# The first two batches of a fused attention and feed-forward kernel: columns of f in runs of four instead of eight

## The chip, the cores and the metric

One core of a Trainium2 chip runs the whole program in one launch. Its engines are TensorE (PE, matrix multiplies), VectorE (DVE), ScalarE (ACT), GpSimd (POOL) and SyncE (SP, which here issues every DMA, in the order of its own queue). The metric is the device time of the launch in microseconds, lower being better. The time before is the median of three runs.

## What is computed

```python
def sm_attn(qq, kk, vv):                    # softmax attention, scale 1/8
    ...
p_packed = sm_attn(p, k, v)                 # 32 packed queries for each head
out      = sm_attn(q, p_packed, p_packed)   # 8 batches, 8 heads, 576 rows, 64 wide
x = out.transpose(0, 2, 1, 3).reshape(4608, 512)
h = x @ w_in                                # 512 -> 2048
g = maximum(h, 0) + alpha * minimum(h, 0)
x = g @ w_out                               # 2048 -> 512
y = (silu(x @ w_gate) * (x @ w_val)) @ w_out2
```

Everything is float32 to the outside. The weights arrive as 64-bit words that the kernel narrows to 32 bits itself, and large products are made of rounded high and low parts in three matmuls.

## The kernel before

There are two stages. The first one goes from q, k, v, p to x after `w_out`, the second is the gated feed-forward. The change lies in the first.

**Units.** A half batch j (288 rows; batch 0 is j = 0 and 1) and a block f of 128 of the 2048 columns make one unit. There are 16 half batches and 16 blocks, so 256 units, numbered `it`. `h_unit` makes the block's h in 6 matmuls, ACT makes `m` (L1003), DVE makes `g` (L1006), ACT rounds it (`hi`, L1014), and POOL takes the rest (`lo`, L1016). Three units later `o_unit` multiplies g into four accumulators `acc` (L1029, L1030, L1035, 12 matmuls), one PSUM bank each, with no second buffer. One DVE instruction on L1006 belongs to each unit, so the rows of L1006 count units.

**Runs.** Consecutive units of one j accumulate in `acc`. When a run ends before f = 15, the sums are copied out (ACT L1051, DVE L1049) and stored to DRAM (`x1p`, SP L1052). The next run of that j loads them back (`load_part`, SP L981) and adds them on DVE as it empties `acc` (L1047). These copies, loads and adds share a pool `x` of two tiles. A run needs both of them, so a load waits until the store of the run ahead has landed. Batches 0 and 1 (j = 0 to 3) go in runs of eight: f 0 to 7 for j = 0, 1, 2, 3 (units 0 to 31), then f 8 to 15 for the same (units 32 to 63). From batch 2 on a run has all sixteen blocks.

**Windows.** h isn't made from x and `w_in` directly: `pp_win(b, j)`, a *window* written `wbj` in the tables, multiplies the packed attention of batch b into four blocks of `w_in` (PE L795 for batches 0 and 1, then an ACT copy and a DVE subtraction, L800, for each half of the heads). It takes two PSUM buffers `at` of which there are two in all. Units of b with f 0 to 3 need window 0, f 4 to 7 window 1, and so on.

**Pieces.** `convert()`, the word `1` in the tables, narrows one of 32 pieces of `w_in` (i0 to i15) and `w_out` (o0 to o15), in the sequence `ORDER`. A piece costs five DVE instructions (L224, L228, L237, L246 and mostly L254), one or two of ACT and one or more of POOL. Window 0 needs i0 to i3, and the units of f need o*f* three units later. Once unit 42 is reached (`GROUP0 = 84`, two slots to a unit), the weights of the second stage are narrowed too, into DRAM (`wgvd`, `wo2d`).

**Order.** `START` and `EARLY` are written by hand: which attention steps (a and b are batch 0, c and d batch 1), pieces and windows stand at which unit. A scheduler makes each engine's queue from that, and each engine works through its queue in order. From unit 32 on each 32 units also carry the attention of the batch that follows.

Of the kernel before, what the change touches and what calls it, by code (L numbers as in the profile page):

```python
# [8 lines left out]
F32 = mybir.dt.float32  # L9
# [8 lines left out]
P = 128  # L18
# [7 lines left out]
LOADS = "b.v a.v 1", "a.q 1 1 b.q"  # L26
START = """
    a.kt0 b.kt0 a.pt a.kt1 b.kt1 b.pt a.s1 a.et a.pp b.s1 a.ppt b.et b.qt0 a.qt0 b.pp b.qt1 a.qt1
    a.s20 b.ppt b.s20 a.a20 b.a20 1 1 1 1 1 w00 1 1
"""  # L30
EARLY = {
    (0, 0): "c.pd d.pd",
    (0, 1): "c.pt 1 b.s21 c.kt0 c.kt1",
    (1, 0): "c.s1",
    (1, 1): "d.kt0 d.pt 1 c.et d.qt0 c.pp",
    (2, 0): "c.qt0",
    (3, 0): "w01 d.qt1 a.s21",
    (3, 1): "c.ppt b.a21",
    (4, 1): "1 d.kt1 d.s1 a.a21 c.qt1",
    (5, 1): "1",  # L40
    (6, 1): "1 d.et",
    (7, 0): "d.pp",
    (7, 1): "1",
    (10, 1): "c.s2 d.ppt d.s2 w10",
    (11, 1): "1",
    (13, 0): "d.a2",
    (15, 0): "c.a2",
    (17, 1): "w11",
    (18, 1): "1 1",
    (20, 1): "1 1",  # L50
    (21, 1): "1",
    (23, 1): "1",
    (24, 1): "1",
    (25, 1): "1 1",
    (26, 1): "1 1",
    (27, 1): "1 w02",
    (28, 1): "w03",
    (33, 1): "1",
    (36, 1): "w12 w13",
    (37, 1): "1 1",  # L60
}

ORDER = """
    i2 o2 i0 i3 i1 o0 o3 o1 i5 i4 i7 i6 o5 o4 o7 o6
    i13 i10 i11 o13 i15 i8 i14 i9 i12 o10 o14 o8 o9 o12 o11 o15
"""

BEHIND = {"c.k": 3, "c.q": 4, "c.v": 5, "d.k": 5, "d.q": 6, "d.v": 9}

BY_POOL = {0, 2, 4, 7, 11, 18, 23, 29}  # L70
HOLD = {15: 5, 16: 7, 17: 15, 19: 16}


STEPS = """
# [12 lines left out]

GROUP0 = 84  # L90


FIRST_X = dict(load=-36, A11=-27, S=-26, S2=-25, A12=-12, D4=-11, S3=-11, S1=-10, A22=-8, S4=-7)
# [11 lines left out]
def f32(ap):  # L105
    return ap.bitcast(F32)
# [3 lines left out]
def tile_kernel(  # L110
# [24 lines left out]
    B, H, S, D = q.shape  # L135
    NP = p.shape[2]
    NT, DM = out.shape
    KC = DM // P
    NF1 = alpha.shape[0] // P
# [6 lines left out]
    HS = S // 2  # L146
    NBLK = NT // (2 * T)
    NQ = H // HQ
    NHALF = 2 * B
# [3 lines left out]
    dram = ctx.enter_context(tc.tile_pool(name="dram", bufs=1, space=DRAM))  # L153
# [16 lines left out]
    def utile(tag, shape, name, dt=F32):  # L170
        return upool.tile(shape, dt, tag=tag, name=name, bufs=UBUFS[tag])
# [32 lines left out]
    def like(ap, other):  # L204

        return ap if len(other.shape) == 2 else ap.rearrange("p (c f) -> p c f", c=KC)
# [4 lines left out]
    def use(*cut):  # L211
        raws[:] = sum((r for r, _ in cut), [])
        vals[:] = sum((v for _, v in cut), [])

    def widen(src, raw, val, out=None, n_piece=-1):
# [3 lines left out]
        low, high = words[:, :, 0], words[:, :, 1]  # L219
        held = n_piece in HOLD  # L220
        with tc.issue_after(begun[HOLD[n_piece]].ins) if held else ExitStack():
            nc.scalar.activation(out=f32(val), in_=f32(high), func=AF.Abs)
# [46 lines left out]
    def convert(n=1):  # L269

        for src, parts, f in queue[:n]:
            raw, val = raws.pop(0), vals.pop(0)
            raws.append(raw)
            vals.append(val)
            n_piece = len(issued)
            dst = parts()
            light = len(dst) == 1
            for _ in widen(src, raw, val, dst[0] if light else None, n_piece):
                pass
            if not light:  # L280
                hi, lo = dst
                full = like(f32(val), hi)
                nc.scalar.activation(out=full, in_=full, func=AF.Copy, scale=sg[:, f : f + 1])
                nc.scalar.activation(out=hi, in_=full, func=AF.Copy)
                nc.gpsimd.tensor_tensor(out=lo, in0=full, in1=f32(hi), op=ALU.subtract)
        del queue[:n]
# [7 lines left out]
    def cut_up(t, raws):  # L294

        n = t.shape[1]
        return (
            [t[:, 1024 * i : 1024 * (i + 1)] for i in range(raws)],
            [t[:, c : c + 512] for c in range(1024 * raws, n, 512)],
        )  # L300
# [248 lines left out]
    def behind():  # L549

        return tc.issue_after(before[-1].ins) if before else ExitStack()

    def done(last):
        if chained:
            before[:] = [last]
# [250 lines left out]
    for f in range(NF1):  # L806
# [4 lines left out]
    space = cut_up(raw_tiles[0], 2), cut_up(raw_tiles[1], 1)  # L811
# [3 lines left out]
        a=quad(0),  # L815
        b=quad(1, ["h"], evac=nc.vector),
        c=quad(2),
        d=quad(3, ["h", "at"]),
# [9 lines left out]
    def run(script):  # L828
        for word in script.split():
            if word == "1":  # L830
                convert()
            elif word[0] == "w":
                pp_win(int(word[1]), int(word[2]))
            else:
                n, step = word.split(".")
                if step == "pd":
                    groups[n][step](pd[:, dense[n][0], :], dense[n][1])
                else:
                    groups[n][step]()

    def alphas():
# [6 lines left out]
        nc.vector.tensor_tensor(out=sal, in0=sg, in1=al, op=ALU.mult)  # L848

    run("a.k")  # L850
    nc.sync.dma_start(out=pd, in_=p[0:2].rearrange("b (g h) n d -> (h n) (b g) d", g=2))
    run("b.k a.pd b.pd")
    for i, words in enumerate(LOADS):
        run(words)
        if i == 0:
            alphas()
    run(START)
    for word, i in BEHIND.items():
        with tc.issue_after(issued[i].ins):
# [6 lines left out]
    def at(it, late, fn):  # L866

        plan.setdefault((it, late), []).append(fn)

    order = []
    for bs in [(0, 1)] + [(b,) for b in range(2, B)]:
        for fs in (range(NF1 // 2), range(NF1 // 2, NF1)) if len(bs) > 1 else (range(NF1),):
            for j in range(2 * bs[0], 2 * bs[-1] + 2):
                order += [(j, f, f == fs[0], f == fs[-1]) for f in fs]

    NB1 = 2 * NF1
    busy = set()
# [3 lines left out]
    for b in range(2, B):  # L883
        d0 = 2 * NB1 * (b - 1)
        steps_of = attention(b)
        for entry in STEPS.split():
            d, names = entry.split(":")
# [74 lines left out]
    def more_weights2(vector):  # L962

        for _ in range(2):
            if not kinds:
                kinds.append(next(work2, None))
            if kinds[0] is None or kinds[0] == "v" and not vector:
                return
            vector = vector and kinds[0] == "p"
            kinds[:] = [next(work2, None)]  # L970
# [5 lines left out]
    x1p = {}  # L976

    def load_part(j):
        part[j] = [utile("x", [P, 2, HS], f"x1p{j}_{pr}") for pr in range(2)]
        for pr in range(2):  # L980
            nc.sync.dma_start(out=part[j][pr], in_=x1p[j][:, 2 * pr : 2 * pr + 2, :])  # L981
# [37 lines left out]
    def o_unit(it):  # L1019
        j, f, start, stop = order[it]  # L1020
        ghi, glo = gs.pop(it)
        hi, lo = wout[f // WP]
        for dc in range(KC):
            if start:
                acc[dc] = ps.tile([P, 512], F32, tag=f"acc{dc}", name=f"acc{dc}_{it}")[:, :HS]
        with behind():
            for dc in range(KC):
                c = slice(dc * P, (dc + 1) * P)
                nc.tensor.matmul(acc[dc], lo[:, f % WP, c], ghi, start=start, stop=False)  # L1029
                last = nc.tensor.matmul(acc[dc], hi[:, f % WP, c], ghi, start=False, stop=False)  # L1030
        done(last)
        with behind():
            for dc in range(KC):
                c = slice(dc * P, (dc + 1) * P)
                last = nc.tensor.matmul(acc[dc], hi[:, f % WP, c], glo, start=False, stop=stop)  # L1035
        done(last)
        if not stop:
            return
        if f != NF1 - 1:
            x1p[j] = dram.tile([P, KC, HS], F32, name=f"x1p{j}")  # L1040
        dst = x1d[j] if f == NF1 - 1 else x1p[j]
        for pr in range(2):
            xs = part[j][pr] if j in part else utile("x", [P, 2, HS], f"x1s{it}_{pr}")
            for i in range(2):
                a = acc[2 * pr + i]
                if j in part:
                    nc.vector.tensor_tensor(out=xs[:, i, :], in0=a, in1=xs[:, i, :], op=ALU.add)  # L1047
                elif i:
                    nc.vector.tensor_copy(out=xs[:, i, :], in_=a)  # L1049
                else:  # L1050
                    nc.scalar.activation(out=xs[:, i, :], in_=a, func=AF.Copy)  # L1051
            nc.sync.dma_start(out=dst[:, 2 * pr : 2 * pr + 2, :], in_=xs)  # L1052

    for j in range(4):
        at(NB1 + 8 * j + 6, 0, lambda j=j: load_part(j))


    raw2, xs2, gvw, wo2, ps2, acc2, outs = {}, {}, {}, {}, {}, {}, {}
# [229 lines left out]
    def steps(it, late):  # L1288


        with ExitStack() as held:
# [6 lines left out]
            slot = 2 * it + late  # L1298
            if slot >= GROUP0:
                more_weights2(slot not in busy)  # L1300
# [59 lines left out]
```

## Time and profile before

| | us |
|---|---|
| median of 3 runs (1701.03 to 1706.88) | 1701.05 |
| profiled execution | 1702.91 |
| its span, first to last instruction | 1701.1 |
| outside the span | 1.8 |

Over the span PE is busy 95%, DVE 51%, ACT 40%, POOL 42%. The average hides that the stretches differ. Until 60.6 us no unit has finished its `g`. The 256 units end at 855 us, the second stage fills the rest. A busy PE isn't PE at its peak: matmuls follow each other every 0.13 us, while the profile gives each about 0.30 us, so a short wait leaves no gap in the row.

### The profile page before, as it was taken

The page shows a single profiled execution, that of the slowest core. Times are in us where ns is not written, and L with a number is a line of the kernel's source. Part 1 is how long each engine was busy: PE and PEld are TensorE (multiplying, and loading weights), DVE is VectorE, ACT ScalarE, POOL GpSimd, SP SyncE. Part 2 cuts the span into 40 slices and gives each one's busy share as a digit, 9 for nine tenths or more (in the row PEclk, how much of TensorE's full clock was granted, in tenths as well). Part 3 has the DMA queues.
Part 4 walks back from the last instruction along what each step waited for, and adds up shares of the span by engine and source line. Part 5 has one row for each costly group of instructions (what it writes and reads, how often), then busy time and mean ns, then how long its engine had stood idle before and what let it go on. Part 6 is the DMA issues. An engine that isn't in the chain of part 4 may idle for free.

```text
span 1701.1 us, 28474 instructions
## 1 busy us (share of the span) xinstructions
PE 1609.9 (95%) x10708; PEld 1456.6 (86%) x10708; DVE 868.2 (51%) x1549; ACT 683.0 (40%) x1511; POOL 708.8 (42%) x752
## 2 busy tenths in 40 slices
PE   5688899999999989999899999999999999999997
PEld 3467798988888888889899999999999999999997
DVE  6999757565756656565533443443443343244222
ACT  5774645555544555454522232232232232123122
POOL 3556744565554654547622322322322222232222
PEclk7799999999999999999999999999999999999999
DMA  9433464635445362644573463465455456445442
GB/s 238 121 102 115 120 159 115 165 95 155 130 108 143 117 156 53 150 138 139 182 274 141 177 237 139 166 202 185 164 211 182 158 191 202 159 174 185 156 173 81
DMA packets 227369, 266.11 MB, mean 156 GB/s; under 512 B 130464, under 2 KB 189856, under 8 KB 227232
## 3 DMA queue, kind: packets, MB, share of 16 engines
q1 hardware_dynamic: 227232, 264.30, 49.2%
q8 instruction: 84, 1.38, 0.3%
q14 instruction: 53, 0.43, 0.1%
HBM read 214.70 MB, written 49.55 MB: 155 GB/s over the span
## 4 chain that ended last, share of the span: by engine, by line
issue 39%; PE 25%; POOL 17%; DMA 7%; DVE 6%; ACT 4%; SPq 1%; POOLq 0%; ACTq 0%; DVEq 0%
POOL pl L1247 8%; PE acc L1029 5%; PE acc L1030 5%; PE acc L1035 5%; POOL s L1227 4%; DMA wgvd<-cva 4%; PE h L305 3%; PE h L307 2%; PE h L306 2%; POOL lo L1016 1%; DMA cva<-in_moe_w_gate_dram 1%; POOL cva L934 1%; DVE g L1006 1%; PE ppw L564 1%; POOL cva L265 1%
## 5 line engine op out<-in xcount | busy, mean ns | idle before, releaser
L1016 POOL TENSOR_TENSOR lo<-g,hi 128x288 fp32r<-128x288 f32 x256 | 227.5, 890 | 240.6 <-ACT hi L1014 187.8
L1227 POOL TENSOR_TENSOR s<-s,u 128x384 f32<-128x384 f32 x72 | 73.0, 1014 | 489.9 <-ACT s L1221 489.9
L1006 DVE SCALAR_TENSOR_TENSOR g<-h,sg,m 128x288 f32<-128x288 f32 x256 | 130.3, 509 | 162.2 <-ACT m L1003 132.0
L1184 DVE TENSOR_TENSOR u<-yb,p 128x384 f32<-128x384 f32 x144 | 80.1, 556 | 255.6 <-PE yb L307 255.6
L1247 POOL TENSOR_TENSOR pl<-s,ph 128x384 fp32r<-128x384 f32 x144 | 145.5, 1032 | 106.4 <-ACT ph L1245 106.4
L305 PE MATMUL h<-a2h,ppw 128*128 128x288 f32 x512 | 163.2, 319 | 27.0 <-DVE g L1006 21.4
L1184 DVE TENSOR_TENSOR u<-vb,u 128x384 f32<-128x384 f32 x144 | 80.4, 558 | 197.3 <-PE vb L307 196.9
L1014 ACT ACTIVATE hi<-g 128x288 fp32r<-128x288 f32 x256 | 113.1, 442 | 155.5 <-DVE g L1006 149.1
L307 PE MATMUL o<-wp,ph 128*128 128x512 f32 x432 | 171.5, 397 | 0.0
L306 PE MATMUL o<-wp,ph 128*128 128x512 f32 x432 | 170.9, 396 | 0.0
L305 PE MATMUL o<-wp,pl 128*128 128x512 f32 x432 | 168.8, 391 | 0.9 <-POOL pl L1247 0.9
L1221 ACT ACTIVATE s<-p 128x384 f32<-128x384 f32 x72 | 37.9, 526 | 302.0 <-DVE p L1184 302.0
L307 PE MATMUL h<-a2l,ppw 128*128 128x288 f32 x512 | 153.0, 299 | 0.0
L306 PE MATMUL h<-a2h,ppw 128*128 128x288 f32 x512 | 152.5, 298 | 0.0
L305 PEld LDWEIGHTS h<-a2h,ppw 128*128 128x128 f32 x512 | 97.9, 191 | 62.4 <-DVE g L1006 33.0
L305 PE MATMUL yb<-ring,gv 128*128 128x384 f32 x432 | 146.0, 338 | 0.2
L307 PE MATMUL yb<-ring,gv 128*128 128x384 f32 x432 | 144.4, 334 | 0.0
L306 PE MATMUL yb<-ring,gv 128*128 128x384 f32 x432 | 144.4, 334 | 0.0
L1003 ACT ACTIVATE m<-h,sal 128x288 f32<-128x288 f32 x256 | 125.6, 492 | 41.5 <-PE h L307 40.6
L1245 ACT ACTIVATE ph<-s 128x384 fp32r<-128x384 f32 x144 | 69.8, 519 | 121.3 <-DVE s L1225 121.3
L307 PEld LDWEIGHTS h<-a2l,ppw 128*128 128x128 f32 x512 | 98.0, 191 | 0.8 <-issue 0.8
L306 PEld LDWEIGHTS h<-a2h,ppw 128*128 128x128 f32 x512 | 98.4, 192 | 0.0
(232 smaller groups left out, 4187.1 us busy)
## 6 DMA issues: line engine op xcount, KB each, us to landing
gv<-wgvd SPq DMA_DIRECT2D x144, 896.0 KB, 6.2
wgvd<-cva SPq DMA_DIRECT2D x84, 256.0 KB, 2.6
cva<-in_moe_w_out_dram SPq DMA_DIRECT2D x28, 512.0 KB, 3.8
v<-in_v_dram SPq DMA_DIRECT2D x16, 576.0 KB, 5.4
out_dram<-os SPq DMA_DIRECT2D x12, 768.0 KB, 3.8
cva<-in_moe_w_in_dram SPq DMA_DIRECT2D x16, 512.0 KB, 3.9
kr<-in_k_dram SPq DMA_DIRECT2D x96, 72.0 KB, 2.8
qr<-in_q_dram SPq DMA_DIRECT2D x96, 72.0 KB, 2.5
```

Source lines behind the costliest of these rows:

```text
L305: nc.tensor.matmul(o, wlo, xhi, start=start, stop=False, **kw)
L306: nc.tensor.matmul(o, whi, xhi, start=False, stop=False, **kw)
L307: return nc.tensor.matmul(o, whi, xlo, start=False, stop=stop, **kw)
L1003: begun[it] = nc.scalar.activation(out=m, in_=hp, func=AF.Copy, scale=sal[:, f : f + 1])
L1006: made[it] = nc.vector.scalar_tensor_tensor(out=g32, in0=hp, scalar=sg[:, f : f + 1], in1=m, op0=ALU.mult, op1=ALU.max)
L1014: rounded[n] = nc.scalar.activation(out=hi, in_=x, func=AF.Copy)
L1016: nc.gpsimd.tensor_tensor(out=lo, in0=x, in1=f32(hi), op=ALU.subtract)
L1029: nc.tensor.matmul(acc[dc], lo[:, f % WP, c], ghi, start=start, stop=False)
L1030: last = nc.tensor.matmul(acc[dc], hi[:, f % WP, c], ghi, start=False, stop=False)
L1184: return nc.vector.tensor_tensor(out=out, in0=bank, in1=x, op=ALU.add)
L1227: latest.append(nc.gpsimd.tensor_tensor(out=s2, in0=s2, in1=u3, op=ALU.mult))
L1247: nc.gpsimd.tensor_tensor(out=lo, in0=x, in1=f32(hi), op=ALU.subtract)
```

## The change

The columns of batches 0 and 1 are taken in other runs, listed in a table `RUNS`. Units 0 to 7 are now f 0 to 3 of j = 0 and 1, units 8 to 15 f 4 to 7 of these. Units 16 to 31 are as before. Units 32 to 47 are f 8 to 11 of j = 0, 1, 2, 3, units 48 to 63 f 12 to 15. A run that isn't the first of its j loads the sums of the run ahead of it, at its own last unit (before: at the seventh of eight). So 10 runs load and add sums where 4 did, and 10 store sums to `x1p` where 4 did.

The tables are rewritten with it. The second half of batch 0's attention (`a.s21`, `a.a21`, `b.a21`) stands some units earlier, since unit 4 uses it now instead of unit 8. Window 1 of batch 0 stands at unit 4 instead of 3, and is needed at unit 8 instead of 4. Windows w03, w12 and w13 stand at units 41, 33 and 50 instead of 28, 36 and 36. The 32 pieces are spread until unit 41 (before: 37). `D` at unit 37 gives up a scratch tile. `GROUP0` is 90, so the second stage's weights begin three units later.

```diff
-    a.s20 b.ppt b.s20 a.a20 b.a20 1 1 1 1 1 w00 1 1
+    a.s20 b.ppt b.s20 a.a20 b.a20 1 1 1 1 1 w00
...
-    (28, 1): "w03",
...
-    (36, 1): "w12 w13",
+    (33, 1): "1 w12",
...
+    (37, 0): "D",
...
+    (41, 1): "1 w03",
...
+    (50, 1): "w13",
...
-    i13 i10 i11 o13 i15 i8 i14 i9 i12 o10 o14 o8 o9 o12 o11 o15
+    i8 i9 i10 i11 o8 o9 o10 o11 i12 i13 i14 i15 o12 o13 o14 o15
...
+RUNS = ((0, 1), 0, 4), ((0, 1), 4, 8), ((2, 3), 0, 8), ((0, 1, 2, 3), 8, 12), ((0, 1, 2, 3), 12, 16)
...
-GROUP0 = 84
+GROUP0 = 90
...
-    order = []
-    for bs in [(0, 1)] + [(b,) for b in range(2, B)]:
-        for fs in (range(NF1 // 2), range(NF1 // 2, NF1)) if len(bs) > 1 else (range(NF1),):
-            for j in range(2 * bs[0], 2 * bs[-1] + 2):
-                order += [(j, f, f == fs[0], f == fs[-1]) for f in fs]
+    order, again = [], []
+    for js, f0, f1 in RUNS + tuple(((j,), 0, NF1) for j in range(4, NHALF)):
+        for j in js:
+            if f0:
+                again.append((len(order) + f1 - f0 - 1, j))
+            order += [(j, f, f == f0, f == f1 - 1) for f in range(f0, f1)]
...
-    for j in range(4):
-        at(NB1 + 8 * j + 6, 0, lambda j=j: load_part(j))
+    for it, j in again:
+        at(it, 0, lambda j=j: load_part(j))
```

Below, names like `g_14` carry the unit; the changed kernel's lines stand 11 to 14 further down (L1049 is L1063, L1047 is L1061, L981 is L995, L1052 is L1066, L795 is L806).

DVE's queue around the end of unit 14, before: `g` of units 14 to 17, pieces in between (`cva`, `cvb`).

```order
L1006 SCALAR_TENSOR_TENSOR g_14_1288<-h_1281,sg,m_1289 128x288
L1006 SCALAR_TENSOR_TENSOR g_15_1325<-h_1318,sg,m_1326 128x288
L224 TENSOR_SCALAR cvb_103<-cvb_103 128x512
L228 TENSOR_SCALAR cvb_103<-cvb_103 128x512
L237 SCALAR_TENSOR_TENSOR cvb_103<-cva_102,cvb_103 128x512
L1006 SCALAR_TENSOR_TENSOR g_16_1352<-h_1345,sg,m_1353 128x288
L224 TENSOR_SCALAR cvb_103<-cvb_103 128x512
L246 TENSOR_SCALAR cva_102<-cvb_103 128x512
L228 TENSOR_SCALAR cvb_103<-cvb_103 128x512
L254 SCALAR_TENSOR_TENSOR cva_102<-cva_102 128x512
L237 SCALAR_TENSOR_TENSOR cvb_103<-cva_101,cvb_103 128x512
L1006 SCALAR_TENSOR_TENSOR g_17_1379<-h_1372,sg,m_1380 128x288
```

The same place of the change, from the last of four additions for the run of units 8 to 11 (`x1p_1_1191`) to the first of four for units 12 to 15 (`x1p_0_1342`):

```order
L1061 TENSOR_TENSOR x1p_1_1191<-acc_8_1236,x1p_1_1191 128x288
L235 TENSOR_SCALAR cvb_103<-cvb_103 128x512
L1020 SCALAR_TENSOR_TENSOR g_15_1353<-h_1346,sg,m_1354 128x288
L239 TENSOR_SCALAR cvb_103<-cvb_103 128x512
L248 SCALAR_TENSOR_TENSOR cvb_103<-cva_102,cvb_103 128x512
L1020 SCALAR_TENSOR_TENSOR g_16_1368<-h_1361,sg,m_1369 128x288
L257 TENSOR_SCALAR cva_102<-cvb_103 128x512
L265 SCALAR_TENSOR_TENSOR cva_102<-cva_102 128x512
L1020 SCALAR_TENSOR_TENSOR g_17_1411<-h_1404,sg,m_1412 128x288
L1061 TENSOR_TENSOR x1p_0_1342<-acc_12_1376,x1p_0_1342 128x288
```

Eight additions stand between `g_14` and `g_18` where two copies stood, the second four only three units behind the first.

SP's queue at that place before, two stores of `x1p` among loads of pieces (`cva`):

```order
L217 DMA cva_101<-in_moe_w_in_dram 128x4x256
L217 DMA cva_102<-in_moe_w_in_dram 128x4x256
L1052 DMA x1p_1455<-x1s_0_1456 128x576
L1052 DMA x1p_1455<-x1s_1_1460 128x576
L217 DMA cva_101<-in_moe_w_in_dram 128x4x256
```

And in the change, where `x1p_7_1325` is the store of the run of units 8 to 11, `x1p_0_1342` and `x1p_1_1343` are the loads for units 12 to 15, and `kr` is batch 2's k:

```order
L1066 DMA x1p_7_1325<-x1p_0_1190 128x576
L603 DMA kr_2_2102<-in_k_dram 32x18x32
L1066 DMA x1p_7_1325<-x1p_1_1191 128x576
L603 DMA kr_2_2102<-in_k_dram 32x18x32 x2
L995 DMA x1p_0_1342<-x1p_3_1181 128x576
L603 DMA kr_2_2102<-in_k_dram 32x18x32
L995 DMA x1p_1_1343<-x1p_3_1181 128x576
```

Between the store of one run and the additions of the next there is now a load that waits for that store.

PE's queue at the windows of batch 1, before, behind the h of unit 36 (`ppw_2` is window 2, `ppw_3` window 3; a row is one half of the heads):

```order
L307 MATMUL h_2085<-a2l_409,ppw_3_1834 128x288
L795 MATMUL ppw_20_2101<-wi_1425,ppT_788 64x512 x2
L795 MATMUL ppw_21_2106<-wi_1425,ppT_1130 64x512 x2
L795 MATMUL ppw_30_2112<-wi_1192,ppT_788 64x512 x2
L795 MATMUL ppw_31_2117<-wi_1192,ppT_1130 64x512 x2
L1029 MATMUL acc_32_2122<-hi_1965,wo2l 128x288
```

In the change, w13 behind the h of unit 50:

```order
L318 MATMUL h_2767<-a2l_409,ppw_3_2360 128x288
L806 MATMUL ppw_30_2783<-wi_1861,ppT_793 64x512 x2
L806 MATMUL ppw_31_2788<-wi_1861,ppT_1143 64x512 x2
L637 MATMUL ppt_2793<-ident,ppbd_94 128x128
L1043 MATMUL acc_44_2682<-hi_2656,wo2l 128x288
```

The two windows of batch 1 stood behind each other and now stand apart, with other work behind each.

## Rows read from the trace of the kernel before

**Rows 1.** Busy time by stretch: length, then busy time and count of each engine.

```profile
core 0: us, PE busy (x) PEld busy (x) DVE busy (x) ACT busy (x) POOL busy (x), PEclk, DMA share, GB/s
60.00:100.00 40.00, 30.14 (x199) 22.87 (x199) 36.75 (x65) 33.57 (x71) 23.44 (x20) 0.96 0.36 108
100.00:140.00 40.00, 36.49 (x258) 29.95 (x257) 35.85 (x63) 24.11 (x54) 25.84 (x23) 1.00 0.31 83
140.00:180.00 40.00, 33.23 (x214) 27.35 (x213) 36.92 (x55) 21.78 (x45) 26.07 (x24) 0.96 0.40 125
180.00:230.00 50.00, 45.00 (x381) 39.48 (x380) 31.91 (x61) 29.16 (x65) 30.07 (x29) 1.00 0.48 125
230.00:286.00 56.00, 55.75 (x508) 49.93 (x507) 37.66 (x69) 28.30 (x64) 29.83 (x34) 1.00 0.58 156
```

**Rows 2.** Waits of DVE, 60 to 180 us: total, times, longest.

```profile
DVE g L1006 <- ACT m L1003: 2.5, 2, 1.9
DVE cvb L224 <- ACT cvb L222: 2.5, 3, 1.5
DVE cva L224 <- ACT cva L222: 2.2, 1, 2.2
```

**Rows 3.** Busy time of L1006 alone (DVE, one a unit), by stretch.

```profile
176.00:286.00 110.00, 18.26 (x37) 1.00 0.52 137
```

**Rows 4.** An addition's duration (min/median/max, ns); then L224, L228, L237, L246, L254 by stretch.

```profile
L1047 DVE TENSOR_TENSOR x1p<-acc,x1p x16: 420/448/457, 223.3 to 295.6; 128x288 f32<-128x288 f32 x16
...
60.00:180.00 120.00, 14.19 (x20) 0.97 0.36 105
...
60.00:180.00 120.00, 17.08 (x20) 0.97 0.36 105
...
60.00:180.00 120.00, 18.16 (x19) 0.97 0.36 105
...
60.00:180.00 120.00, 12.19 (x20) 0.97 0.36 105
...
60.00:180.00 120.00, 14.99 (x17) 0.97 0.36 105
```

**Rows 5.** Timeline of DVE: start, duration; `g` of units 14 and 17.

```profile
131.65 0.50 DVE L1006 SCALAR_TENSOR_TENSOR g<-h,sg,m 128x288 f32<-128x288 f32 x1
...
138.96 0.50 DVE L1006 SCALAR_TENSOR_TENSOR g<-h,sg,m 128x288 f32<-128x288 f32 x1
```

**Rows 6.** Timelines of DVE and SP at three run ends, then L981's time to landing.

```profile
192.48 0.82 DVE L1049 COPY x1s<-acc 128x288 f32<-128x288 f32 x2 [0.24 <-PE acc L1035]
...
199.34 0.48 SPq L981 DMA_DIRECT2D x1p<-x1p  x1
...
223.33 1.54 DVE L1047 TENSOR_TENSOR x1p<-acc,x1p 128x288 f32<-128x288 f32 x4
...
226.31 1.09 SPq L981 DMA_DIRECT2D x1p<-x1p  x2
...
245.16 1.55 DVE L1047 TENSOR_TENSOR x1p<-acc,x1p 128x288 f32<-128x288 f32 x4
...
249.79 1.69 SPq L981 DMA_DIRECT2D x1p<-x1p  x2
...
DMA to landing us min/median/max: 2.7/3.3/5.4
```

**Rows 7.** Timeline of PE at windows w12 and w13; in brackets the idle time ahead.

```profile
200.04 1.08 PE L795 MATMUL ppw<-wi,ppT 128*64 128x512 f32 x4 [3.05 <-DVE ppw L800]
```

**Rows 8.** Timeline of ACT near the end of the second stage's weights.

```profile
841.05 0.42 ACT L933 ACTIVATE cva<-cva 128x256 fp32r<-128x256 f32 x1 [3.18 <-DMA wgvd<-cva]
```

**Rows 9.** Durations on L228 over the whole span, min/median/max in ns.

```profile
L228 DVE TENSOR_SCALAR cva<-cva x50: 386/426/1539, 16.5 to 828.9; 128x512 uint32<-128x512 uint32 x50
```

**Rows 10.** Waits of PE, 60 to 180 us: total, times, longest.

```profile
PE acc L1029 <- DVE x1s L1049: 3.0, 1, 3.0
```

More of the change, by code (lines that the diff above doesn't have):

```diff
@@ L32 @@
     (0, 0): "c.pd d.pd",
-    (0, 1): "c.pt 1 b.s21 c.kt0 c.kt1",
+    (0, 1): "c.pt 1 b.s21 a.s21 c.kt0 c.kt1",
     (1, 0): "c.s1",
[L35 to L40, printed above, removed]
+    (1, 1): "1 b.a21 d.kt0 d.pt",
+    (2, 0): "a.a21 c.et",
+    (2, 1): "1 c.pp",
+    (3, 0): "d.qt0",
+    (3, 1): "1 c.qt0",
+    (4, 1): "c.ppt d.kt1 w01",
+    (5, 1): "1 d.s1 c.qt1",
     (6, 1): "1 d.et",
     (7, 0): "d.pp",
-    (7, 1): "1",
+    (7, 1): "1 d.qt1",
+    (8, 1): "1",
     (10, 1): "c.s2 d.ppt d.s2 w10",
@@ L48 @@
     (17, 1): "w11",
-    (18, 1): "1 1",
-    (20, 1): "1 1",
+    (18, 1): "1",
+    (20, 1): "1",
     (21, 1): "1",
@@ L53 @@
     (24, 1): "1",
-    (25, 1): "1 1",
-    (26, 1): "1 1",
-    (27, 1): "1 w02",
-    (28, 1): "w03",
-    (33, 1): "1",
-    (36, 1): "w12 w13",
-    (37, 1): "1 1",
+    (25, 1): "1",
+    (26, 1): "w02",
+    (27, 1): "1",
+    (29, 1): "1",
+    (31, 1): "1",
+    (33, 1): "1 w12",
+    (34, 1): "1",
+    (35, 1): "1",
+    (36, 1): "1",
+    (37, 0): "D",
+    (39, 1): "1",
+    (41, 1): "1 w03",
+    (43, 1): "1",
+    (50, 1): "w13",
 }
@@ L64 @@
     i2 o2 i0 i3 i1 o0 o3 o1 i5 i4 i7 i6 o5 o4 o7 o6
-    i13 i10 i11 o13 i15 i8 i14 i9 i12 o10 o14 o8 o9 o12 o11 o15
+    i8 i9 i10 i11 o8 o9 o10 o11 i12 i13 i14 i15 o12 o13 o14 o15
 """
-BEHIND = {"c.k": 3, "c.q": 4, "c.v": 5, "d.k": 5, "d.q": 6, "d.v": 9}
+BEHIND = {"c.k": 3, "c.q": 4, "c.v": 5, "d.k": 5, "d.q": 6, "d.v": 7}
 BY_POOL = {0, 2, 4, 7, 11, 18, 23, 29}
-HOLD = {15: 5, 16: 7, 17: 15, 19: 16}
+HOLD = {17: 15, 19: 18}
+RUNS = ((0, 1), 0, 4), ((0, 1), 4, 8), ((2, 3), 0, 8), ((0, 1, 2, 3), 8, 12), ((0, 1, 2, 3), 12, 16)
 STEPS = """
@@ L831, in run @@
                 convert()
+            elif word == "D":
+                use(*space)
             elif word[0] == "w":
@@ L1039, in o_unit @@
         if f != NF1 - 1:
-            x1p[j] = dram.tile([P, KC, HS], F32, name=f"x1p{j}")
+            x1p[j] = dram.tile([P, KC, HS], F32, name=f"x1p{j}_{f}")
         dst = x1d[j] if f == NF1 - 1 else x1p[j]
```

## The prediction

> **What bounds the kernel now.** I read the busy times by stretch first [rows 1]. The reader is to see two regimes ahead of 286 us. From 60 to 180 us DVE is busy 36.75 + 35.85 + 36.92 = 109.5 of 120 us, 91%, while PE is at 99.9 of 120. From 230 us on PE is busy 55.75 of 56 us and DVE only 37.66. So DVE sets the pace of units 0 to about 28, PE that of the rest, and the stretch from 180 to 230 is the passage between them. Then I read whom DVE waits for in its own stretch [rows 2]: the longest entries are ACT's `m` (2.5 us) and ACT's first step of a piece (2.5 and 2.2 us). All its idle time there is 120 - 109.5 = 10.5 us, which is the most that any rearrangement ahead of 180 us can take from idle time on DVE without shortening its work. The question for the change is therefore how much DVE work stands ahead of each unit.
>
> **DVE's work ahead of the units.** The change lets pieces be needed later, but what counts is where they stand in DVE's queue. I counted the finished pieces (fifth instruction, L246) ahead of `g` in both orders: ahead of unit 0 it is 8 before and 8 now, of unit 4 15 and 13, of unit 8 17 and 17, of unit 16 19 and 19, of unit 28 27 and 26, of unit 40 32 and 30. The relief at unit 4 is eaten by unit 8, where batch 0's second half of attention now comes earlier. At unit 28, where DVE's regime ends, one piece is left over. A piece costs, summed over its five lines in this stretch [rows 4], 14.19/20 + 17.08/20 + 18.16/19 + 12.19/20 + 14.99/17 = 0.71 + 0.85 + 0.96 + 0.61 + 0.88 = 4.0 us. Against it stand eight additions that weren't there (second runs of j = 0 and 1) at 0.45 us each [rows 4], 3.6 us. First term: 3.6 - 4.0 = **-0.4 us**. The copies of the first runs are as many as before (four runs, two DVE copies each), only earlier. The piece left over, and the 16 other additions (16 x 0.45 = 7.2 us), fall behind 180 us, where DVE has 50 - 31.91 + 56 - 37.66 = 36 us idle [rows 1]; I cost them at nothing, and at 7.2 us if that cover were gone.
>
> **The loop through DRAM.** New is a loop: additions empty `acc`, their tile is stored, the store must land, the next run's sums are loaded into the same tile, and the next additions wait for them. While they wait, `acc` is full, and PE, which has no second accumulator, holds the next run's `o_unit`; behind it in its queue stand all later units, so all engines stop. Before, the loop had eight units of time. Its length can be read at three run ends [rows 6], from the first copy or addition to the issue of the last load, plus that load's landing: from 223.33 to 227.1 (the second of two issues in 1.09 us, each about 0.3) plus the median 3.3, 7.1 us; from 245.16 to 251.2 plus 3.3, 9.3 us; and from 192.48 to 199.34 plus the longest, 5.4, 12.3 us, because SP had five loads of k and v in between.
>
> At units 12 to 15 the additions now stand three units behind those of units 8 to 11 in a queue where unit 17 followed unit 14 after 138.96 - 131.65 = 7.3 us [rows 5], and SP's queue has loads of k between them, as at the longest of the three. So they come late by something between 0 and 12.3 - 7.3 = 5 us, and DVE, the bound there, waits. By the middle loop, 9.3 us, it is 2 us. Second term: **+2 us**, bounds 0 and 5.
>
> In units 32 to 63 eight loops have four units each. There 37 units take 110 us [rows 3], four of them 11.9 us. Two of the three loops fit with 2.6 us or more to spare, the third is late by 0.4 us. Units don't come evenly, though: at the fastest pace seen, three in 7.3 us [rows 5], four take 9.7, and the longest loop would be late by 2.6 us. I take one late loop in three, by some 0.75 us between 0 and 2.6 that is nearer the mean pace: 8/3 x 0.75 = **+2 us**, bounds 0 and 8 x 2.6 = 21. The Trainium skill bears on this loop ("DMA: Bandwidth & Descriptors", section "Anatomy of one DMA"): it puts a transfer at about 2.0 us fixed plus its bytes at 436 GB/s, by which I estimate 2.7 us for each of the 295 KB moved here; a store and a load would make 5.4 us, every loop would hide, and the sum would be 2 us less in the last term and 2 us less in the second. The landings of the loads agree at their shortest, 2.7 us, and not at their longest, 5.4.
>
> **The windows.** Before, w12 and w13 stand behind each other, and PE stood idle 3.05 us because the first one's two `at` buffers weren't yet emptied by DVE [rows 7]. In the new order each window has other matmuls behind it, so the wait is gone, in a stretch where PE is the bound. Third term: **-3 us**; the bound above is 0, if the time is lost to the next thing late, which is `g` of the unit.
>
> **The second stage's weights.** They begin three units later and end two units later in POOL's queue. ACT already waits for one of their stores near the end, 3.18 us [rows 8], and in my reading that wait moves with them; 0, bounds 0 and +3.2 if it comes a second time. But for a few rows, PE's queue is the same from unit 70 on.
>
> **The sum.** -0.4 + 2 + 2 - 3 + 0 = +0.6 us. Against the profiled execution, 1702.91 us, that is 1703.5. That execution lies 1.86 us above the median of the runs, so the forecast for the median is 1701.05 + 0.6, rounded to **1702 us**. With the loops hidden (-0.4 - 3) it is 1698; with a late second run (5), twice the late loops (4) and no gain at the windows it is 1701 + 5 + 4 - 0.4 = 1710: that is the likeliest case's own range. A measurement of this kernel can tell about 0.5%, 8.5 us, from no change, so this is no change, chance 0.52.
>
> **Rivals.**
>
> *Slower: the loop becomes the bound.* If SP's queue (loads of k, q, v, pieces, and stores of second-stage weights that wait for POOL) makes the loop 12.3 us as a rule and units come at the fast pace, the eight loops cost up to 21 us and the second term 5: 1701 + 21 + 5 - 3.4 = 1725 us; half of it, 1713. It decides from a mean lateness of (8.5 + 3.4 - 2)/8 = 1.2 us a loop on. For it speaks the loop of 12.3 us; against it that two of three are under 9.4. A run end with a full DVE queue has also cost 3.0 us of PE once [rows 10], and there are two such ends more, but PE isn't the bound there. Chance 0.22.
>
> *Faster: DVE's waits go.* If the looser needs let ACT run ahead with the pieces, so that DVE never waits before 180 us, the 10.5 us go and with them the 3 us at the windows: 1701 - 10.5 - 3.4 + 2 = 1689 us. For it: 4.7 us of these waits are for ACT's first step of a piece. Against: the pieces stand about where they stood, and raw tiles are as many. Chance 0.17.
>
> *Faster: DVE's instructions get shorter.* In DVE's stretch L228 averages 0.85 us [rows 4], while its median over the span is 0.43 on the larger group [rows 9]; if pieces now met less of POOL's work, L228 alone would give 20 x (0.85 - 0.43) = 8.4 us and the others as much again at most, some 1685 to 1693 us. Against: POOL's rows ahead of unit 16 are as many as before. The Trainium skill's "SBUF — State Buffer", section "Who interferes with whom", names such a lock, on a port pair that DVE and GpSimd share, taken for a whole instruction; the spread of L228's durations, 386 to 1539 ns, agrees with a lock. Chance 0.09.
>
> **Range and chances.** Faster by over 0.5% is the two rivals, 0.26; slower 0.22; within 0.5% 0.52. The range reaches into both sides until about 0.2 is left out: 1688 to 1718, which takes a good half of either rival.
>
> **What would show it.** Right: unit 28's `g` near 176 us, within 4; DVE about 91% busy from 60 to 180 us; no idle of PE over 1 us ahead of L806; additions (L1061) that wait for a load (L995) at units 17 or so, by about 2 us, and one or two more later. Wrong: PE idle at `acc` in most of the runs of four (the loop binds), or `g` of unit 28 ahead of 168 us (DVE's waits or durations shrank). A difference in the second stage, whose PE order is unchanged, would be outside this account.

## The result, and the profile after

The changed kernel takes 1718.92 us (median of 4 runs, 1717.32 to 1720.9) against 1703.97 us of the kernel before (4 runs, 1701.03 to 1709.1): ratio 1.0092, interval 1.0071 to 1.0114, so 0.92% slower, 15.7 us by the ratio and 15.0 by the two medians. Two more comparisons on other chips gave 1.0113 and 1.0096. The forecast was 1702 us with a range of 1688 to 1718. Its span is 1718.1 us.

Busy time by stretch, in the columns of [rows 1]:

```profile
60.00:100.00 40.00, 33.57 (x196) 24.72 (x196) 35.24 (x66) 31.11 (x69) 23.67 (x21) 0.86 0.35 109
100.00:140.00 40.00, 35.06 (x227) 28.04 (x228) 29.08 (x60) 26.97 (x58) 22.82 (x21) 0.91 0.42 122
140.00:180.00 40.00, 36.04 (x246) 31.29 (x244) 35.28 (x56) 21.50 (x45) 26.57 (x23) 1.00 0.43 128
180.00:230.00 50.00, 40.47 (x277) 34.98 (x277) 36.23 (x61) 24.57 (x55) 28.93 (x27) 0.93 0.53 137
230.00:286.00 56.00, 50.78 (x475) 45.07 (x474) 33.75 (x67) 23.92 (x55) 24.20 (x29) 0.94 0.55 159
```

Two things are new. DVE lost 6.8 us of work between 100 and 140 us (29.08 busy, 35.85 before). And from 180 us on, where PE is the bound, PE is busy 4.5 and 5.0 us less, with a granted clock of 0.93 and 0.94 where both stretches had 1.00 before. Fewer units get through, 32 where [rows 3] have 37:

```profile
176.00:286.00 110.00, 15.97 (x32) 0.94 0.53 148
```

By the starts of `g`, counted in both traces, 3.6 us are lost up to unit 32, and from unit 32 to unit 80 it takes 159.8 us where it took 143.9 (158.4 and 158.0 in two further executions of the change). From unit 80 on nothing more is lost.

PE's waits from 190 to 300 us (total, times, longest) name the new stalls. First before, where the window of [rows 7] is the longest, then after:

```profile
PE ppw L795 <- DVE ppw L800: 3.5, 2, 3.0
PE h L305 <- DVE g L1006: 3.5, 3, 2.6
...
PE ppt L637 <- DVE ppw L811: 5.0, 1, 5.0
PE s L575 <- DVE ppw L811: 2.4, 2, 2.1
PE h L316 <- DVE g L1020: 2.4, 4, 0.8
PE s L575 <- DVE kT L625: 2.0, 1, 2.0
```

No `acc` stands in the list after, nor does it up to 330 us, behind the last addition (310.7 us), so no run of four made PE wait for an accumulator. L811 is the subtraction that empties a window's `at` buffers. PE's timeline shows what stands behind the two moved windows, w03 at unit 41 and w13 at unit 50:

```profile
218.56 0.60 PE L806 MATMUL ppw<-wi,ppT 128*64 128x512 f32 x2
221.22 0.71 PE L575 MATMUL s<-kT,pT 64*32 64x288 f32 x8 [2.06 <-DVE ppw L811]
222.31 1.19 PE L575 MATMUL s<-kT,pT 64*32 64x288 f32 x8 [0.38 <-DVE ppw L811]
...
250.75 1.94 PE L806 MATMUL ppw<-wi,ppT 128*64 128x512 f32 x8
257.67 0.47 PE L637 MATMUL ppt<-ident,ppbd 128*128 128x128 f32 x1 [4.98 <-DVE ppw L811]
...
258.19 0.44 PE L1044 MATMUL acc<-hi,wo2h 128*128 128x288 f32 x1
258.43 0.44 PE L1043 MATMUL acc<-hi,wo2l 128*128 128x288 f32 x1
```

Behind w03 stand the logits `s` of batch 2's attention, behind w13 its transpose `ppt`, and both want the two `at` buffers that the window has just filled. At w03 DVE works off a piece and a `g` and comes to the subtraction only at 220.49, though ACT's copy was done at 219.16. For w13, DVE, SP and ACT tell why the emptying came so late:

```profile
254.99 0.43 DVE L235 TENSOR_SCALAR cva<-cva 128x512 f32<-128x512 f32 x1 [6.34 <-ACT cva L233]
255.44 0.52 DVE L1020 SCALAR_TENSOR_TENSOR g<-h,sg,m 128x288 f32<-128x288 f32 x1
255.87 0.42 DVE L239 TENSOR_SCALAR cva<-cva 128x512 uint32<-128x512 uint32 x1
256.32 0.69 DVE L248 SCALAR_TENSOR_TENSOR cva<-cva 128x512 uint32<-128x512 uint32 x1
256.93 1.28 DVE L811 TENSOR_TENSOR ppw<-ppw,ppw 128x512 fp32r<-128x512 f32 x2
...
246.57 1.17 SPq L995 DMA_DIRECT2D x1p<-x1p  x2
247.97 0.38 SPq L228 DMA_DIRECT2D cva<-in_moe_w_val_dram  x1
248.45 0.46 SPq L618 DMA_DIRECT2D v<-in_v_dram  x1
...
254.29 0.66 ACT L233 ACTIVATE cva<-cva 128x512 f32<-128x512 f32 x1 [5.17 <-DMA cva<-in_moe_w_val_dram]
...
255.24 0.60 ACT L810 ACTIVATE ppw<-ppw 128x512 fp32r<-128x512 f32 x1
```

A piece of the second stage's weights (`w_val`, 512 KB) is issued at 247.97, between two loads of partial sums (288 KB each) and a load of `v` (576 KB), and lands 6.3 us later. ACT waits for it, DVE's next instruction waits for ACT, 6.34 us idle, and w13 stands behind that piece in both queues: its copies (L810) on ACT and its subtractions (L811) on DVE.

The granted clock, in steps of 2 us around both stalls (length, PE busy, clock, DMA):

```profile
220.00:222.00 2.00, 0.71 (x8) 0.94 0.79 126
222.00:224.00 2.00, 1.69 (x10) 0.50 0.84 237
224.00:226.00 2.00, 2.00 (x11) 0.50 0.08 26
226.00:228.00 2.00, 2.00 (x10) 0.50 0.00 0
...
258.00:260.00 2.00, 2.00 (x10) 0.50 0.00 0
260.00:262.00 2.00, 2.00 (x10) 0.50 0.00 0
262.00:264.00 2.00, 2.00 (x24) 0.82 0.78 295
```

After each stall PE works for some 5 to 6 us at the lower of its two levels (0.50, 1.2 GHz): its matmuls start every 0.24 us there, where 0.13 is the pace otherwise. So a stall has a second price. The steps at 0.50 shown, 222 to 228 and 258 to 262, hold 5.69 + 4.00 us of work; by my estimate half of it, 4.8 us, is lost to the clock. The windows' bill after is then 2.06 + 0.38 + 4.98 + 4.8 = 12.2 us, against 3.05 before, when the clock stayed at 1.00 [rows 1].

Ahead of 180 us, two lines of DVE's timeline. The first is the longest new gap, the second the additions at unit 17, which waited for PE's last matmul of that run (L1049):

```profile
112.11 0.43 DVE L235 TENSOR_SCALAR cvb<-cvb 128x512 f32<-128x512 f32 x1 [4.90 <-ACT cvb L233]
...
143.66 1.55 DVE L1061 TENSOR_TENSOR x1p<-acc,x1p 128x288 f32<-128x288 f32 x4 [1.32 <-PE acc L1049]
```

### The profile page after: what moved, and what is told of

Same layout as the page of the kernel before. It is cut to its first block, busy times and chain, and to the rows that moved or that the text cites. A ratio compares the mean times of both kernels' runs of the same rounds, so it can differ in the third digit from the quotient of the medians.

```text
span 1718.1 us, 28541 instructions
## 1 busy us (share of the span) xinstructions
PE 1618.2 (94%) x10708; PEld 1461.4 (85%) x10708; DVE 871.1 (51%) x1573; ACT 682.7 (40%) x1511; POOL 704.4 (41%) x752
## 4 chain that ended last, share of the span: by engine, by line
issue 39%; PE 20%; POOL 17%; DMA 10%; DVE 7%; ACT 4%; SPq 2%; POOLq 0%; ACTq 0%; DVEq 0%
POOL pl L1261 8%; POOL s L1241 4%; PE acc L1043 4%; DMA wgvd<-cva 4%; PE acc L1044 3%; PE acc L1049 3%; PE h L316 2%; PE h L318 2%; PE h L317 2%; POOL cva L276 2%; DMA cva<-in_moe_w_gate_dram 1%; POOL lo L1030 1%; DMA cva<-in_moe_w_val_dram 1%; POOL cva L948 1%; DVE g L1020 1%
## 5 line engine op out<-in xcount | busy, mean ns | idle before, releaser
L1028 ACT ACTIVATE hi<-g 128x288 fp32r<-128x288 f32 x256 | 112.9, 442 | 147.7 <-DVE g L1020 143.9
L316 PE MATMUL xb<-ring,gv 128*128 128x384 f32 x288 | 96.3, 334 | 2.9 <-DMA gv<-wgvd 2.9
```

What stands on the lines that cost most here:

```text
L316: nc.tensor.matmul(o, wlo, xhi, start=start, stop=False, **kw)
L1028: rounded[n] = nc.scalar.activation(out=hi, in_=x, func=AF.Copy)
```

## Experiments

Every ratio is against the kernel before on the same chip, with its 95% interval. "Windows clear" means w03 at unit 38 and w13 at unit 47.

**First half alone**: RUNS, START and the entries of EARLY up to unit 16 as in the change, with the smaller tables that belong to them (HOLD without its first two entries, BEHIND); the rest as before.

```diff
-RUNS = ((0, 1), 0, 4), ((0, 1), 4, 8), ((2, 3), 0, 8), ((0, 1, 2, 3), 8, 12), ((0, 1, 2, 3), 12, 16)
+RUNS = ((0, 1), 0, 4), ((0, 1), 4, 8), ((2, 3), 0, 8), ((0, 1, 2, 3), 8, 16)
-GROUP0 = 90
+GROUP0 = 84
```

> Only the first batch's first eight columns go in two runs of four; units 32 to 63 keep the runs, the windows and the start of the second stage's weights of the kernel before. In the trace of the full change g of unit 16 is 4.3 us late, of unit 28 5.3 us. Theory 1 (two separate losses: DVE's queue idles about 9 us more ahead of unit 28, and PE then waits 8.2 us at the two windows w03 and w13): 4 to 6 us over the kernel before. Theory 2 (all of it is the loop through DRAM in units 32 to 63 and what it crowds out of SP's queue): no more than 2 us over the kernel before.

Measured: 1.0014 (1.0000 to 1.0029), 2.4 us, so less than theory 1 had for this half and at the edge of theory 2.

**Second half alone**: units 0 to 31 as before, then the change's runs of four, windows and GROUP0.

```diff
-RUNS = ((0, 1), 0, 4), ((0, 1), 4, 8), ((2, 3), 0, 8), ((0, 1, 2, 3), 8, 12), ((0, 1, 2, 3), 12, 16)
+RUNS = ((0, 1, 2, 3), 0, 8), ((0, 1, 2, 3), 8, 12), ((0, 1, 2, 3), 12, 16)
```

> Only the last eight columns of the first two batches go in two runs of four, with the windows, pieces and start of the second stage's weights of the change from unit 17 on; units 0 to 16 are those of the kernel before. Theory 1: 9 to 12 us over the kernel before, with a wait of PE for the subtraction of a window (L811) of 2 us or more at w03 and again at w13. Theory 2: 13 to 16 us over, most of it at additions that wait for a load.

Measured: 1.0059 (1.0041 to 1.0077), 10 us. PE's waits are those of the whole change: 5.5 us at `ppt`, 2.5 at `s` behind a window. Most of the loss lies in this half, as theory 1 had it.

**Windows clear**, the whole change otherwise:

```diff
+    (38, 1): "w03",
-    (41, 1): "1 w03",
+    (41, 1): "1",
+    (47, 0): "w13",
-    (50, 1): "w13",
```

> The full change, with w03 moved from unit 41 to 38 and w13 from the end of unit 50 to the start of 47, where batch 2's attention steps don't ask for the two PSUM buffers named at in the slots beside them. Theory 1: the waits of 3.0 and 5.2 us there go, 6 to 9 us faster than the full change (1718.9), that is 1710 to 1713. Theory 2: within 2 us of the full change, since runs, loads and additions are the same.

Measured: 1.0026 (1.0012 to 1.0040). Run again beside the whole change on another chip:

> The changed kernel with both windows moved (w03 to unit 38, w13 to unit 47), again, beside the changed kernel on one chip. Theory: 0.006 to 0.008 below the changed kernel's ratio. Rival, the difference seen before came from two chips: less than 0.004 below it.

> The changed kernel once more, as the measure on this chip for the three that follow. Both theories: ratio 1.008 to 1.012.

Measured: 1.0038 (1.0023 to 1.0053) and 1.0096 (1.0073 to 1.0119), so 0.0058 less, just under what was expected: 9.9 us of 1705.64, by the two intervals 5 to 15. From unit 32 to unit 80 the two executions take 147.9 and 147.5 us, so 12 of the 15.9 us lost there are back. PE's waits in the second one, 190 to 300 us, then its row of busy time by stretch:

```profile
PE h L317 <- DVE g L1021: 3.8, 6, 1.4
PE et L690 <- ACT E L670: 1.2, 1, 1.2
PE s L576 <- ACT E L658: 0.6, 1, 0.6
```

```profile
230.00:286.00 56.00, 54.53 (x510) 47.96 (x499) 40.11 (x80) 27.86 (x63) 27.42 (x32) 1.00 0.65 179
```

No wait for a window is left (0.4 us in the first execution), and the clock is back at 1.00. Also gone is the wait of 2.0 us for `kT`: w03 now stands where PE waited for it. In the change DVE's transposition of `kT` (211.62 us) stood behind four additions (209.83, 1.54 us); without them (next experiment) that wait is 0.5 us. So these additions weren't hidden.

**No loads**: the whole change, but the partial sums of the earlier runs are neither loaded nor added, so the output lacks them.

```diff
-                again.append((len(order) + f1 - f0 - 1, j))
+                pass
```

> The full change without loading and adding the sums of the runs ahead: each run's sums are copied out and stored, so x is made of the last run alone; 20 loads and 40 additions are left out, half of the copies that replace the additions are ACT's. Theory 2 (the loop): 10 to 15 us faster than the full change, near the kernel before. Theory 1: 3 to 6 us faster, for the additions and SP's shorter queue, while the window waits at about 221 and 257 us stay.

Measured: 1.0027 (1.0012 to 1.0043), as with the windows clear on that chip, and by its size what theory 2 had. That alone would read as if the loops through DRAM were the cost. The trace names another wait that went: the one at `ppt` behind w13 is 0.8 us there (at w03 2.0 stays), since the same `w_val` piece lands after 3.6 us instead of 6.3:

```profile
241.43 0.38 SPq L228 DMA_DIRECT2D cva<-in_moe_w_val_dram  x1
```

Both kernels mend the same wait, one by moving the window, one because the load lands sooner. What of the rest of this gain is the additions', the trace doesn't split.

The partial sums aren't the main reason why that load takes 6.3 us. In five traces with w13 at unit 50 and `GROUP0` 90 (the change three times, the second half alone, w03 alone) the load of `v` follows 0.5 us behind, and `w_val` takes 5.9 to 6.8 us. In four with w13 at unit 47 (both windows twice, w13 alone, the second half with windows clear) the same two loads of partial sums stand ahead, but `v` follows only 2.4 us behind, as it does without the loads, and `w_val` takes 4.3 to 4.6 us. The rows of w13 alone, 4.3 us:

```profile
245.63 1.03 SPq L995 DMA_DIRECT2D x1p<-x1p  x2
247.37 0.38 SPq L228 DMA_DIRECT2D cva<-in_moe_w_val_dram  x1
249.76 0.33 SPq L618 DMA_DIRECT2D v<-in_v_dram  x1
```

So some 0.7 to 1.0 us go with the partial sums and the larger part with the load of `v`. Moving w13 also moved that load.

**Whole change again, and w13 alone**, on one chip. The edit of the second is the last two lines of the windows' diff.

> The changed kernel as it is, so that the next three runs have it beside them on one chip. Both theories: 14 to 17 us over the kernel before, ratio 1.008 to 1.010.

> The changed kernel with only w13 moved, from unit 50 to unit 47 (w03 stays at 41). Theory 1, the windows' waits are the cost, and the longer one is w13's (5 us at the ppt step): 5 to 8 us less than the changed kernel, ratio 1.004 to 1.006, with the stall of 2 to 3 us at w03 still in the trace. Rival, the late load of w_val is the cost and w13 only shows it: the wait turns up at another instruction of PE, and the ratio stays at 1.008 to 1.010.

Measured: 1.0113 (1.0096 to 1.0130) and 1.0081 (1.0066 to 1.0096). The wait at `ppt` is gone and the one at w03 stays, 2.3 us, as expected. The gain, 0.0032 or 5.5 us, is of the size expected (by the two intervals 2 to 9); from unit 32 to unit 80 it is 152.4 us against 158.0. The ratio itself lies where the rival had it, because the measure beside it came out higher than thought, but the wait turns up at no other instruction of PE, against the rival. Since `w_val` lands sooner here too, this run doesn't part the two; `GROUP0` 84 alone, below, does.

**w03 alone**, on the chip of the third run of the whole change:

> The changed kernel with only w03 moved, from unit 41 to unit 38 (w13 stays at 50). Theory: PE's waits of 2.2 to 2.4 us ahead of s at w03 go, 2 to 5 us less than the changed kernel (ratio 0.001 to 0.003 less), and the wait at ppt behind w13 stays. Rival, moving w13 alone gave too little for the sum, so w03's move also takes the wait at w13 away (the second stage's loads come at other times): ratio 0.004 or more below the changed kernel's.

Measured: 1.0086 (1.0067 to 1.0105), 0.001 below the change, at the lower edge of the theory and within the uncertainty, so no run shows by its time what w03 alone costs. In the trace it is 155.3 us from unit 32 to unit 80, against 158.4. The wait behind w13 stays:

```profile
PE ppt L638 <- DVE ppw L812: 4.9, 1, 4.9
```

**GROUP0 84 alone**, the windows where the change has them:

```diff
-GROUP0 = 90
+GROUP0 = 84
```

> The changed kernel with one edit, GROUP0 84 in place of 90; the windows stay at units 41 and 50. In the order of DVE no step of a piece stands between g of unit 49 and the subtractions of w13 then, while the ppt step still stands behind w13 on PE. Theory, the late piece ahead of the subtractions makes the wait: PE's wait at ppt behind w13 falls from 5 us to under 1.5 us, and the ratio is 0.002 to 0.004 below that of the changed kernel. Rival, the two at buffers make it whatever stands on DVE: 3 us or more of it stays, and the ratio is within 0.0015 of the changed kernel's.

Measured: 1.0058 (1.0037 to 1.0079), 0.0038 below the change (by the two intervals 0.0007 to 0.0069). PE's waits, 190 to 300 us, then DVE's timeline at w13:

```profile
PE h L316 <- DVE g L1020: 5.2, 6, 1.5
PE s L575 <- DVE ppw L811: 2.4, 2, 2.0
...
PE ppt L637 <- DVE ppw L811: 0.7, 1, 0.7
```

```profile
254.95 1.51 DVE L811 TENSOR_TENSOR ppw<-ppw,ppw 128x512 fp32r<-128x512 f32 x2 [0.63 <-ACT ppw L810]
```

Window and transpose stand as in the change, and the wait falls from 5.4 (the change on that chip) to 0.7 us. So the shared `at` buffers by themselves cost some 0.7 us here; the rest came from the piece that stood ahead of the copies and subtractions. In this execution PE's waits for `g` are 5.2 us, where the change on that chip has 3.3.

**Second half alone, windows clear**, with GROUP0 90 and then 84:

> Second half of the change alone (units 0 to 31 as before, runs of four in units 32 to 63), with w03 at unit 38 and w13 at unit 47. Theory 1: without the two waits at the windows the second half costs only its additions, which are hidden, so -2 to +3 us, ratio 0.999 to 1.002. Rival, the loads of partial sums among the other loads cost by themselves: at least half of what the second half cost with its own windows stays, ratio 1.003 to 1.006.

> Second half of the change alone with w03 at unit 38 and w13 at unit 47, and the second stage's weights beginning at unit 42 as before (GROUP0 84). Theory: the later beginning (GROUP0 90) costs what these kernels lose between units 64 and 255 (6.6 us with the windows clear), so unit 255 keeps its lead of unit 64, ratio 0.996 to 0.999, faster than the kernel before. Rival, these losses are not of GROUP0: ratio 0.9995 to 1.001, as with GROUP0 90.

Measured: 1.0001 (0.9989 to 1.0013) and 0.9994 (0.9985 to 1.0004). Runs of four with their eight loops, loads and additions cost nothing that can be told, once the windows are out of the way. The start of the second stage's weights isn't a cost of its own: the theory on GROUP0 fell. So it did in the whole change with the windows clear and GROUP0 84:

> The whole change with w03 at unit 38 and w13 at unit 47, and GROUP0 84 as before. Theory: what is left is the first half's cost, so 2 to 4 us less than with GROUP0 90, ratio 1.000 to 1.002. Rival, GROUP0 costs nothing: ratio 1.002 to 1.004.

Measured: 1.0029 (1.0018 to 1.0040), against 1.0026 and 1.0038 with 90.

**The windows of the kernel before, apart**:

```diff
-    (33, 1): "1",
-    (36, 1): "w12 w13",
+    (33, 1): "1 w12",
+    (36, 1): "w13",
```

> The kernel before with one edit: w12 at unit 33 and w13 at unit 36, where both stood at unit 36. Theory 1, a window costs a wait only where the next user of the two at buffers stands right behind it: the wait of 3.05 us goes, 2 to 4 us less than before, ratio 0.9975 to 0.999. Rival, the time goes to the next thing late (g of the unit): no wait at the window, and ratio 0.9995 to 1.001.

Measured: 1.0024 (1.0010 to 1.0037), a loss of 4 us. The 3.05 us of [rows 7] are gone, and PE waits elsewhere, first in PE's timeline, then what it waits for in POOL's:

```profile
212.72 0.61 PE L1029 MATMUL acc<-hi,wo2l 128*128 128x288 f32 x1 [6.47 <-POOL wo2l L285]
213.12 0.44 PE L1030 MATMUL acc<-hi,wo2h 128*128 128x288 f32 x1
...
211.40 1.27 POOL L285 TENSOR_TENSOR wo2l<-cva,wo2h 128x512 fp32r<-128x512 f32 x1 [0.25 <-ACT wo2h L284]
```

PE reached this `o_unit` before its piece of `w_out` was ready. Without the second window there it was through with the `h` ahead some 3 us sooner than before (206.2 us, before 209.3), and the piece was done 2.9 us later (212.67, before 209.82), of which 1.7 us is how late this execution is at unit 32 anyway. Its matmuls came at the slow pace behind that stall too (0.44 us each). Neither answer on record held: the wait went to the next thing late, as the rival said, but at twice the price.

**The first half's holds.** The change also dropped two entries of HOLD, by which ACT's first step of a piece waits until another piece has begun.

```diff
-HOLD = {17: 15, 19: 16}
+HOLD = {15: 5, 16: 7, 17: 15, 19: 16}
```

> The first half of the change alone (as in the first experiment), with the table HOLD as before: the first steps of pieces 15 and 16 on ACT are held back again until pieces 5 and 7 have begun, which the change had dropped. Theory: without these holds two pieces run interleaved ahead of g of unit 7, the raw tile of the next one comes free late, and DVE idles 4.9 to 5.9 us at 110 to 113 us; with them the gap falls under 2 us, and unit 16 comes 3 to 5 us earlier than in the first experiment, ratio 0.998 to 1.000. Rival, the pieces wait for raw tiles whatever their order: the idle time turns up elsewhere ahead of unit 16, ratio 1.001 to 1.003.

Measured: 1.0009 (0.9996 to 1.0023). DVE's gap of the first half alone, and the one that took its place:

```profile
112.62 0.43 DVE L228 TENSOR_SCALAR cvb<-cvb 128x512 f32<-128x512 f32 x1 [5.85 <-ACT cvb L226]
```

```profile
105.54 0.52 DVE L1013 SCALAR_TENSOR_TENSOR g<-h,sg,m 128x288 f32<-128x288 f32 x1 [4.05 <-ACT m L1010]
```

The rival held: the idle time moved. All three edits together (windows clear, GROUP0 84, holds) gave no more either. The ratio is in the rival's range, but its reason isn't shown by it, since the second half with its loops costs nothing:

> The whole change with all three edits: w03 at unit 38 and w13 at unit 47, GROUP0 84, and the holds of pieces 15 and 16 as before; the runs of four stay in both halves. Theory: each part of the loss is undone, ratio 0.996 to 1.000. Rival, the runs of four cost by themselves (loops through DRAM, additions): ratio over 1.002 still.

Measured: 1.0023 (1.0013 to 1.0033). No version was measurably faster than the kernel before.

## Why the prediction was wrong

**The step that failed is the third term.** "In the new order each window has other matmuls behind it, so the wait is gone": -3 us, bound 0. Other matmuls do stand behind them, but the shown rows of PE's queue went only as far as `ppt` and `acc`, and I didn't ask which PSUM buffer each wants. `ppt` and `s` want `at`. I also didn't ask what stands ahead of the window's copies and subtractions in the queues of ACT and DVE: a piece whose load was still under way. By the rows the term is 12.2 - 3.05 = +9 us, and moving the two windows gave 9.9 us back (5 to 15), with the wait for `kT` among them. That is 12 to 13 of the some 15 us between the forecast and the result. The bound of 0 was wrong as well, as the kernel before with its windows apart shows: the next thing late cost more than the wait removed.

**The clock** stood in no term. The Trainium skill ("TensorE: Matmul & The Clock Gate", section "Part 1: The HAM clock gate") says that the lower level is where PE falls back to when idle, and that activity releases it. The rows at 222 and 258 us agree; the wait of 3.05 us before, at a granted clock of 1.00, shows no fall. By the estimate above it was worth some 4.8 of the 12.2 us.

**DVE's work ahead of the units** (-0.4) and **the late second run** (+2). The sum of the two, +1.6, against 2.4 us measured for the first half alone (interval 0 to 5): the size was right, by luck. The additions at unit 17 did come 1.3 us late, but they waited for PE's `acc` and not for a load (L995), and no addition in the trace did. The first term's reason fails too. The pieces ahead of each unit are as many as counted (on L246, which is the fourth of a piece's five instructions), but DVE doesn't stay busy between them: 29.08 of 40 us between 100 and 140, with one gap of 4.90 us that is there before any partial sum is loaded. I had costed DVE's work and taken its idle time as fixed. From 60 to 180 us DVE was 83% busy, not 91%. `g` of unit 28 came at 181.00, 1 us outside the 176 ± 4 given.

**The loops in units 32 to 63** (+2, bounds 0 and 21) cost nothing: PE never waits for `acc` behind an addition, and the second half with the windows clear is at 1.0001. The time from issue to landing of these loads, 2.6/3.2/6.1 us at least, median and most, is about that of [rows 6]; the loops had that time. By the estimate from the Trainium skill ("DMA: Bandwidth & Descriptors", section "Anatomy of one DMA"), whose fit is for transfers that GpSimd issues and not SyncE as here, every loop would hide, and they did. So the Slower rival had the sign right and its mechanism wrong: the loop did not become the bound. (Its sum, 1701 + 21 + 5 - 3.4, is 1724, not 1725.) What the loads and additions did is indirect, and no rival had it: the loads stood ahead of a piece's load in the same queue (some 0.7 to 1.0 of its 6.3 us), and four additions, costed at nothing, stood ahead of `kT` (some 1.5 us).

**The second stage's weights** (0): ACT's waits for their stores near the end are 2.04 and 2.38 us, where [rows 8] have 3.18, and GROUP0 moved no ratio with the windows clear. So 0 holds by the time, but the weights' lateness moved from ACT to PE, which now waits for a load of them at the start of the second stage:

```profile
PE xb L316 <- DMA gv<-wgvd: 2.9, 1, 2.9
```

All ten traces with GROUP0 90 have this wait, 0.8 to 2.9 us, and none of the eight with 84; it is too small for the ratios to price. Where the windows stay, GROUP0 matters, by the place of one piece at w13.

**The two Faster rivals** didn't come. DVE's waits grew: it idled 20.4 of the 120 us from 60 to 180, where it had idled 10.5. L239 (L228 of before) took 14.06 us for 18 there, 0.78 each, where it had 0.85.

**What stays open**: with windows clear the whole change still costs 0.0023 to 0.0038, and the first half alone 0.0009 to 0.0014, while the second alone costs nothing. So some 2 to 4 us aren't accounted for; the two traces with windows clear are 2.1 and 3.2 us late at unit 32, lose some 4 more up to unit 80, and nothing behind it. Why DVE idles some 4 to 6 us ahead of unit 8 with either table of holds isn't settled: the holds moved the gap and didn't close it. That the `w_val` load lands late because of the load of `v` close behind it is read from nine executions in which that load also stands elsewhere; a kernel that moves this load alone, or the partial sums into another queue, wasn't tried.

## What to carry to other kernels

When a step is moved, look up which buffer each instruction behind it wants and what its releasing instruction queues behind; "other work follows" is no answer if that work takes the same two buffers. On an engine that is the bound, price a stall with the slow clock behind it, here about two thirds of the stall again by estimate (and nothing in the kernel before). When leaving something out gives the time back, read which wait went: here taking out the loads and moving a window cured the same 5 us.

## Unexpected on the chip

A wait of 3.05 us before left the granted clock at 1.00; waits of 4.98 us, and of 2.06 us some 9 us after another of 2.0, were followed by some 5 to 6 us at 0.50. In the kernel with GROUP0 84 alone the same two waits of 2.0 us cost less clock (0.97 over 180 to 230 us, 0.93 in the change). The 512 KB load of `w_val` took 5.9 to 6.8 us to land with a 576 KB load issued 0.5 us behind it, and 4.3 to 4.6 with that load 2.4 us behind, both with two loads of partial sums ahead; without those it took 3.6.
